# Loading the exponential's table behind the last square root of the gMLP, in a decode kernel that streams a key and value cache

## The chip, the core and the metric

The kernel runs on one core of a Trainium2 chip. The metric is the device time of one execution in microseconds (us). Before the change the median was 664.88 us of 3 runs (664.66 to 665.18).

## The reference

One layer norm, then two branches that are added to the input. Branch A is attention of one query per batch row over a cache of 4096 positions. Branch B is a small gMLP. The exponential (softmax), the GELU and the square roots (layer norms) are what the change is about.

```python
xn = _layernorm(x)                                   # a square root
q  = (xn @ wq)            # B=4, H=32, Dh=128
p  = softmax(q @ k_cache^T * Dh**-0.5)               # exponentials; k_cache 4 x 32 x 4096 x 128 bf16
A  = (p @ v_cache) @ wo
z  = gelu(xn @ w_in)                                 # GELU
z2 = _layernorm(z[..., Fh:])                         # a second square root
B  = (z[..., :Fh] * (w_sp * z2 + b_sp)) @ w_out
return x + A + B
```

The two caches are 134 MB each.

## The kernel before

The cache is cut into 16 key units and 16 value units of 8.39 MB (4 groups of 8 heads, 4 batch rows). They pass through five slots of on-chip memory, two slots to a unit, on one transfer queue: the four key units of the first group come first, then value and key units in turn. VectorE transposes a key unit in 8 steps (L361), TensorE makes the scores. After the fourth key unit of a group comes the softmax of the group, then TensorE multiplies with the value units. A new unit is issued when what lay in its slots has been used.

```python
# end of the gMLP (L316 to L332, cut)
nc.scalar.activation(out=rs[:], in_=var[:], func=ACT.Sqrt, bias=eps_t[:, 0:1], scale=1.0)   # L322
nc.vector.reciprocal(out=rs[:], in_=rs[:])                                                    # L323
# ... four more VectorE operations
etab = const.tile([P, 1], F32)
nc.scalar.activation(out=etab[:], in_=eps_t[:], func=ACT.Exp)                                 # L332

def softmax(g):
    negmax = softmax_max(g)            # row maxima: VectorE, one TensorE step, VectorE
    # ...
    for e in range(NE):                # L415
        nc.scalar.activation(out=p_bf[:, :, e, :], in_=S_ps[:, e], func=ACT.Exp, bias=negmax[:, e:e + 1], ...)
    # transpose, copies, z_fill(g, 0), z_fill(g, 1): the weights Zb of the value matmuls

def emit_V(v):                         # L444
    nc.tensor.matmul(O_ps[...], lhsT=Zb[b % 2][...], rhs=vv[...], ...)     # 64 of them
```

In the trace a table load (ACT_TABLE_LOAD) stands in front of an activation wherever the kind of function changes: square root (6.44 us), exponential (8.05), GELU (24.47), square root (26.48), exponential (122.59). None stands before the copies or before the exponentials of the later softmaxes. etab is read by nothing: it is there to have the exponential's table loaded early. The instructions are ordered by a scheduler that moves what is ready early to the front.

## Time and profile before

| | before |
|---|---|
| span of the profiled execution | 662.6 us |
| transfers | 282.25 MB, 426 GB/s over the span |
| VectorE, TensorE, ScalarE busy | 55%, 44%, 12% |
| table loads on ScalarE | 5 of 1.28 us |
| first softmax: exponential starts | 123.88 us |
| first value matmul, issue of the next value unit | 132.35, 136.00 us |

### The profile page before, as it was taken

To read this page: it belongs to the slowest core of one execution; us is meant where nothing else is said; L and a number is where in the kernel's file an instruction comes from. 1 tells how busy PE (TensorE), PEld (TensorE's weight loads), DVE (VectorE), ACT (ScalarE), POOL (GpSimd) and SP (SyncE) were. 2 spreads that over 40 slices of the span, in tenths; PEclk is the share of its full clock that TensorE was granted. 3 is DMA by queue.
4 is the path that set the end of the run, shared out by engine and by line. 5 is a ranking of instruction groups with operands and counts; after the bars stand their busy time and mean duration, and the time that the engine had idled before them with its cause. 6 is when DMAs were issued, how large, how long until landed. Compare 5 with 4: busy or idle time off the path is not lost.

```text
span 662.6 us, 5430 instructions
## 1 busy us (share of the span) xinstructions
PE 294.1 (44%) x2283; PEld 106.3 (16%) x2283; DVE 362.5 (55%) x340; ACT 79.5 (12%) x163; POOL 10.8 (2%) x35
## 2 busy tenths in 40 slices
PE   0525566266072556225446055633506254623245
PEld 0201122022021122111112022111202112211012
DVE  4338999656190849609265286745618084950002
ACT  1200000541100000530200000071110000052200
POOL 3000000000000000000000000000000000000000
PEclk9858968668577587677758596755958659667767
DMA  9999999999999999999999999999999999999996
GB/s 374 459 440 432 404 434 445 443 428 436 420 427 440 435 413 448 431 431 432 431 444 427 435 416 432 448 435 428 423 436 443 432 435 407 437 436 441 424 413 262
DMA packets 6901, 282.61 MB, mean 427 GB/s; under 512 B 808, under 2 KB 1084, under 8 KB 1500
## 3 DMA queue, kind: packets, MB, share of 16 engines
q1 hardware_dynamic: 6856, 282.25, 98.8%
q8 instruction: 18, 0.29, 0.2%
q14 instruction: 7, 0.06, 0.0%
q10 hardware_dynamic: 20, 0.01, 0.0%
HBM read 282.25 MB, written 0.01 MB: 426 GB/s over the span
## 4 chain that ended last, share of the span: by engine, by line
DMA 74%; DVE 11%; issue 11%; PE 2%; ACT 1%; SPq 0%; DVEq 0%; ACTq 0%
DMA kv<-in_A_k_cache_dram 63%; DVE kT L361 11%; DMA kv<-in_A_v_cache_dram 5%; DMA kv<-in_A_wo_dram 3%; DMA kv<-in_A_wq_dram 2%; PE O L444 2%; ACT xd L426 0%; ACT Zb L407 0%; SPq L169 0%; ACT p L415 0%; PE last_a L542 0%; DVE pT L419 0%; DVE m L379 0%; PE S L372 0%; PE misc L384 0%
## 5 line engine op out<-in xcount | busy, mean ns | idle before, releaser
L361 DVE STREAM_TRANSPOSE kT<-kv 128x2048 f32<-128x2048 f32 x128 | 282.8, 2275 | 128.5 <-DMA kv<-in_A_k_cache_dram 128.5
L372 PE MATMUL S<-kT,QZ 128*32 128x512 bf16 x1024 | 190.8, 506 | 233.3 <-DVE kT L361 233.3
L372 PEld LDWEIGHTS <-QZ 128*32 128x32 bf16 x1024 | 61.0, 111 | 357.6 <-issue 337.9
L444 PE MATMUL O<-kv,Zb 128*32 128x512 bf16 x1024 | 75.2, 458 | 58.1 <-DMA kv<-in_A_v_cache_dram 37.9
L451 DVE TENSOR_SCALAR R<-O,Mk 128x128 f32<-128x128 f32 x16 | 5.6, 351 | 122.8 <-PE O L444 122.8
L407 ACT ACTIVATE Zb<-xd,MkE 32x256 bf16<-32x256 bf16 x116 | 52.9, 498 | 108.3 <-PE O L444 106.9
L444 PEld LDWEIGHTS <-Zb 128*32 128x32 bf16 x1024 | 33.0, 113 | 99.6 <-issue 58.5
L415 ACT ACTIVATE p<-S,negmax 128x512 bf16<-128x512 f32 x8 | 5.4, 682 | 311.6 <-DVE negmax L393 311.6
L461 PE MATMUL misc<-R,SelR 128*32 128x128 f32 x32 | 6.4, 281 | 26.2 <-DVE R L453 26.2
L453 DVE SCALAR_TENSOR_TENSOR R<-O,Mk,R 128x128 f32<-128x128 f32 x48 | 16.8, 351 | 1.7
L426 DVE COPY xd<-pT 32x256 bf16<-32x256 bf16 x44 | 16.0, 364 | 0.8
L426 ACT COPY xd<-pT 32x256 bf16<-32x256 bf16 x20 | 12.2, 612 | 5.6 <-DVE pT L419 5.2
L415 ACT ACT_TABLE_LOAD x1 | 1.3, 1283 | 93.1 <-DVE negmax L393 93.1
L347 POOL COPY QZ<-qT 32x32 bf16<-32x32 bf16 x16 | 5.1, 316 | 413.4 <-PE S L372 399.8
L419 DVE STREAM_TRANSPOSE pT<-p 128x1024 bf16<-128x1024 bf16 x4 | 5.0, 1245 | 7.6 <-ACT p L415 7.6
L379 DVE TENSOR_REDUCE m<-S 128x2 f32<-128x1024 f32 x4 | 4.9, 1225 | 5.6 <-PE S L372 5.6
L461 PEld LDWEIGHTS misc<-R,SelR 128*32 128x32 f32 x32 | 2.2, 107 | 34.0 <-DVE R L453 25.3
L268 PE MATMUL q<-kv,xnT 128*32 128x512 bf16 x40 | 4.5, 631 | 5.2 <-DMA kv<-in_A_wq_dram 5.2
L384 PE MATMUL misc<-dg,ones_f 128*128 128x256 f32 x8 | 3.2, 491 | 7.5 <-DVE dg L381 7.5
L464 DVE SCALAR_TENSOR_TENSOR om<-misc,rinv,MkH 32x1024 bf16<-32x1024 f32 x4 | 5.1, 1272 | 2.0 <-PE misc L461 2.0
L430 PE MATMUL misc<-rowsum,SelP 128*32 128x2 f32 x8 | 1.1, 204 | 11.3 <-ACT p L415 11.3
L276 DVE CAST kv<-q 128x512 bf16<-128x512 f32 x1 | 0.7, 692 | 9.5 <-PE q L268 9.5
(102 smaller groups left out, 73.3 us busy)
## 6 DMA issues: line engine op xcount, KB each, us to landing
kv<-in_A_k_cache_dram SPq DMA_DIRECT2D x8, 4096.0 KB
kv<-in_A_v_cache_dram SPq DMA_DIRECT2D x1, 6144.0 KB
kv<-in_A_wq_dram SPq DMA_DIRECT2D x1, 5120.0 KB
kv<-in_A_wo_dram SPq DMA_DIRECT2D x3, 1280.0 KB
kv<-in_B_w_in_dram SPq DMA_DIRECT2D x1, 2160.0 KB, 19.9
kv<-in_A_v_cache_dram SPq DMA_DIRECT2D x1, 2048.0 KB
kv<-in_B_w_out_dram SPq DMA_DIRECT2D x1, 960.0 KB
kv<-in_A_wo_dram SPq DMA_DIRECT2D x1, 640.0 KB, 21.7
```

The source lines that it names most:

```text
L347: nc.gpsimd.tensor_copy(out=QZ[r0:r0 + 32, :, :, :, 8 + 8 * hp], in_=qT[32 * g:32 * g + 32, NE * hp:NE * hp + NE].rearrange("p e a b -> p ...
L361: nc.vector.transpose(kT[:].rearrange("p (t r) -> p t r", r=32), kw)
L372: nc.tensor.matmul(S_ps[32 * q:32 * q + 32, e], lhsT=QZ[:, b, 2 * kh + w, e, w0:w0 + 32], rhs=kb[:, i, :, e, :, w], start=(b == 0 and k < ...
L407: nc.scalar.activation(out=dst, in_=src, func=ACT.Copy, scale=mk)
L415: nc.scalar.activation(out=p_bf[:, :, e, :], in_=S_ps[:, e], func=ACT.Exp, bias=negmax[:, e:e + 1], scale=scale, accum_out=rowsum[:, e:e + 1])
L419: nc.vector.transpose(pT[:].rearrange("p t h x -> p (t h x)"), p_bf[:].rearrange("p t e m -> p (t e m)"))
L426: op(out=xd[32 * hp:32 * hp + 32, :, q, :], in_=pT[32 * q:32 * q + 32, :, hp, :].rearrange("p t x -> p x t"))
L444: nc.tensor.matmul(O_ps[32 * q:32 * q + 32, :, :], lhsT=Zb[b % 2][:, w].rearrange("p h c -> p (h c)"), rhs=vv[:, w * 4 * Dh:(w + 1) * 4 * ...
L451: nc.vector.tensor_scalar(out=R, in0=O_ps[:, 0, :], scalar1=Mk4[:, 0:1], scalar2=None, op0=ALU.mult)
L453: nc.vector.scalar_tensor_tensor(out=R, in0=O_ps[:, c, :], scalar=Mk4[:, c:c + 1], in1=R, op0=ALU.mult, op1=ALU.add)
L461: nc.tensor.matmul(oh[:], lhsT=SelR[:, b].rearrange("p h b -> p (h b)"), rhs=state["R"][:, b, :], start=(b == 0), stop=(b == B - 1))
L464: nc.vector.scalar_tensor_tensor(out=om[:], in0=oh[:, None, :].to_broadcast((G, HG, Dh)), scalar=state.pop(("rinv", g))[:, 0:1], in1=MkH[: ...
```

## The change

The intent is to have the exponential's table in place before the first softmax, where its load stood on the chain from the last scores to the first value matmul. etab reads rs, so it can't run before the second square root.

```diff
     etab = const.tile([P, 1], F32)
-    nc.scalar.activation(out=etab[:], in_=eps_t[:], func=ACT.Exp)
+    nc.scalar.activation(out=etab[:], in_=rs[:], func=ACT.Exp, scale=1e-3)
```

## The prediction

> **What bounds the kernel now.** I read the page first (busy shares and the 40 slices), then the chain that ended last, then every ScalarE instruction in order of time, and last the issue and landing times of the cache transfers around the first softmax, which is where the change acts.
>
> The page of the kernel before:
>
> ```profile
> DMA  9999999999999999999999999999999999999996
> HBM read 282.25 MB, written 0.01 MB: 426 GB/s over the span
> DMA 74%; DVE 11%; issue 11%; PE 2%; ACT 1%; SPq 0%; DVEq 0%; ACTq 0%
> ```
>
> The DMA row is at 9 in every slice but the last, so the 16 DMA engines are moving data from the first to the last slice. ScalarE is 1% of the chain. The bytes set the time: 282.25 MB at 426 GB/s are 662.6 us, the whole span. A change that moves no bytes can help only where the transfer queue runs dry, at the head, or in the tail behind the last transfers.
>
> ScalarE in order of time, kernel before (start, duration, engine, line, operation; in brackets the idle time before it and what ended it):
>
> ```profile
> 6.44 1.28 ACT L195 ACT_TABLE_LOAD   x1 [6.44 <-DVE ssq L193]
> 7.74 0.29 ACT L195 ACTIVATE rstd<-ssq,eps_t 4x1 f32<-4x1 f32 x1
> 8.05 1.28 ACT L332 ACT_TABLE_LOAD   x1
> 9.34 0.20 ACT L332 ACTIVATE etab<-eps_t 128x1 f32<-128x1 f32 x1
> 21.24 0.59 ACT L276 CAST kv<-q 128x512 bf16<-128x512 f32 x1 [11.69 <-DVE kv L276]
> 24.47 1.28 ACT L297 ACT_TABLE_LOAD   x1 [2.65 <-PE misc L291]
> ...
> 26.48 1.28 ACT L322 ACT_TABLE_LOAD   x1
> 29.21 0.29 ACT L322 ACTIVATE rs<-var,eps_t 128x1 f32<-128x1 f32 x1 [1.45 <-DVE var L319]
> 122.59 1.28 ACT L415 ACT_TABLE_LOAD   x1 [93.08 <-DVE negmax L393]
> 123.88 0.69 ACT L415 ACTIVATE p<-S,negmax 128x512 bf16<-128x512 f32 x1
> ```
>
> This shows what the author of the change saw. The preload of the exponential's table (etab, L332) stands in the source behind the gMLP, but its input eps_t is ready early, so it ran at 8.05 us, ahead of the GELU and of the second square root. Each of these loads its own table, so the exponential's is gone by 29.5 us. It is loaded again at 122.59 us, inside the first softmax, with the row maximum (negmax) done and everything waiting for the exponential. Five loads in all; no later softmax has one.
>
> **What the Trainium skill says.** "ScalarE: Activation LUTs", section "What ACT_TABLE_LOAD costs": about 1283 ns for the load and about 1380 ns for a drain, together 2.66 us for each switch of set. The trace agrees with 1283 ns (1.28 us in all five) but shows no drain beside it: negmax ends at 122.51, the load runs from 122.59 to 123.87, the exponential starts at 123.88. I use 1.28 to 1.29 us. The same page, "Table sets: the hidden batching unit", puts exp and sqrt into different sets and copies into every set. The trace agrees: the CAST at 21.24 and the copies between the later softmaxes have no load. So with etab behind the last square root nothing on ScalarE should evict the exponential's table again.
> "DMA: Bandwidth & Descriptors", section "Bandwidth", measures 425 GB/s for one large load and puts the fabric ceiling at 435 GB/s. The 426 GB/s here is at that level. (The page's 358 GB/s for HBM per core is passed here, so the measurement decides.) I therefore expect no idle bandwidth to win.
>
> **The change, part by part.**
> 1. Removed at 8.05 us: one load and one 0.20 us activation, 1.49 us of ScalarE from 8.05 to 9.54. ScalarE next has work at 21.24, which waits for VectorE. Worth 0 us.
> 2. Added behind the second square root: etab now reads rs, which the reciprocal (L323, 29.54 to 29.71) finishes. A wait on one engine did not hold back the load of L322 (it ran at 26.48, the activation waited 1.45 us more), so I expect the load at about 29.5 to 30.8 and etab of 0.20 us at about 30.8 to 31.0. ScalarE is idle from 29.5 to 122.59, and the gMLP's remaining path (L324 to L340) is VectorE and TensorE only. Nothing reads etab. Worth 0 us.
> 3. Removed at 122.59: the load in the first softmax. Four loads stay instead of five. The exponential can start at about 122.59 instead of 123.88: the softmax, the filling of Zb and the first value matmuls (132.35 us) come 1.29 us earlier. This is the only gain, and the question is whether it reaches the end.
>
> What waits for these matmuls is the issue of the next value transfer, which overwrites half of the first value unit. The trace in order of time, kernel before:
>
> ```profile
> 132.35 6.02 PE L444 MATMUL O<-kv,Zb 128*32 128x512 bf16 x64 [6.71 <-ACT Zb L407]
> ...
> 136.00 0.33 SPq L161 DMA_DIRECT2D kv<-in_A_v_cache_dram  x1
> ...
> 140.78 17.66 DVE L361 STREAM_TRANSPOSE kT<-kv 128x2048 f32<-128x2048 f32 x8 [0.84 <-DMA kv<-in_A_k_cache_dram]
> ...
> 149.70 0.33 SPq L161 DMA_DIRECT2D kv<-in_A_k_cache_dram  x1
> ...
> 160.16 3.64 PE L444 MATMUL O<-kv,Zb 128*32 128x512 bf16 x64 [0.55 <-DMA kv<-in_A_v_cache_dram]
> ...
> 179.77 17.66 DVE L361 STREAM_TRANSPOSE kT<-kv 128x2048 f32<-128x2048 f32 x8 [14.42 <-DMA kv<-in_A_k_cache_dram]
> ```
>
> The value transfer is issued at 136.00 while the key unit before it is still arriving; that lands at about 140.76. So the queue has 4.76 us of work left. The value unit lands at about 160.14, 19.4 us after the key unit; the next key unit, issued 10.4 us before its predecessor landed, lands 19.6 us after it (179.75). A unit of 8.39 MB at 427 GB/s needs 19.6 us, by calculation. The value unit lost nothing to its late issue. Issued at 134.7 it has 6.05 us of slack instead of 4.76 and lands when it did before. The sum over the three parts: 0 us.
>
> The finer windows agree: from 120 to 160 us in steps of 5 us the DMA share is 0.97 to 1.03 and the rate 410 to 446 GB/s, no dip.
>
> **The rivals.**
> a) The 1.29 us reaches the end. For it: the chain in the first softmax really is serial from the last key matmul to the first value matmul. Against it: after that the chain that ended last contains the key transfers at 108.67 to 140.76 and 149.70 to 179.75, not this softmax; and no softmax but the first had a load, so the exposed last softmax (580.6 to 593.8 us in the chain) gets nothing. Time: 664.88 - 1.29 = 663.6; with the skill's full 2.66 us it would be 662.2.
> b) The transfer issued earlier collides with the key unit in flight, which lands later, by up to the 1.29 us. For it: two transfers on the same 16 engines. Against it: the same bytes go through the same engines, and the next key issue (149.70) that hangs on that unit has 10.4 us of slack. Time: unchanged, 664.9.
> c) The new dependency makes the scheduler arrange other instructions differently, at the head above all, or puts the load in front of something that waits. For it: etab was already moved once by readiness. Against it: ScalarE has nothing else to do from 29.5 to 122.6. Where the head is touched, a loss of at most the load and etab, 1.5 us, could follow: 666.4.
> d) The load is not saved because an activation between 31 and 122 us takes another set. Nothing in the trace is there. Time: 664.9.
>
> **Range and chances.** The centre is the time before less a tenth for the small chance of (a): 664.8. The three runs before spread over 0.52 us. I allow for (a) at the low end and for another chip session and part of (c) at the high end: 663.6 to 665.9. A change of 2% would be 13.3 us, ten times the only duration that the change touches; I give 1% to each side.
>
> **What would show it right or wrong.** Right: four table loads, one of them with L332 at about 29.5 us; no load at L415; the first exponential at about 122.6; the first value matmul near 131.1; the value transfer issued near 134.7; and yet the value unit landing near 160.1 and everything after it within some tenths of where it was. Wrong at step 2: etab still early, or its load waiting on the path of L324. Wrong at step 3: the landing near 160.1 and the key landings after it (179.75, 218.46) move forward by about 1.3 us, which would mean that the queue was short of work where I read it as full.

## The result and the profile after

The changed kernel took 664.61 us (median of 6 runs, 664.48 to 664.67), the kernel before 664.85 us (6 runs, 664.40 to 665.18). The ratio is 0.9996 with a 95% interval of 0.9984 to 1.0009: the same.

The page of the changed kernel:

```profile
DMA  9999999999999999999999999999999999999996
HBM read 282.25 MB, written 0.01 MB: 426 GB/s over the span
DMA 74%; DVE 11%; issue 11%; PE 2%; ACT 1%; SPq 0%; DVEq 0%; ACTq 0%
```

The three lines are those of before to the last digit. ScalarE in order of time, changed kernel:

```profile
6.45 1.28 ACT L195 ACT_TABLE_LOAD   x1 [6.45 <-DVE ssq L193]
...
24.68 1.28 ACT L297 ACT_TABLE_LOAD   x1 [2.82 <-PE misc L291]
...
26.68 1.28 ACT L322 ACT_TABLE_LOAD   x1
29.42 0.29 ACT L322 ACTIVATE rs<-var,eps_t 128x1 f32<-128x1 f32 x1 [1.45 <-DVE var L319]
29.73 1.28 ACT L332 ACT_TABLE_LOAD   x1
31.03 0.20 ACT L332 ACTIVATE etab<-rs 128x1 f32<-128x1 f32 x1
122.93 0.69 ACT L415 ACTIVATE p<-S,negmax 128x512 bf16<-128x512 f32 x1 [91.70 <-DVE negmax L393]
```

The change did what it was meant to do. Four loads instead of five, the exponential's directly behind the square root, and none at L415. The order of the instructions on all other engines is the same in both kernels, but for a few TensorE records near 264 us that trade places.

The stretch around the first value matmul in order of time, changed kernel:

```profile
131.40 6.01 PE L444 MATMUL O<-kv,Zb 128*32 128x512 bf16 x64 [6.71 <-ACT Zb L407]
135.05 0.33 SPq L161 DMA_DIRECT2D kv<-in_A_v_cache_dram  x1
...
140.78 17.66 DVE L361 STREAM_TRANSPOSE kT<-kv 128x2048 f32<-128x2048 f32 x8 [1.79 <-DMA kv<-in_A_k_cache_dram]
...
160.15 3.64 PE L444 MATMUL O<-kv,Zb 128*32 128x512 bf16 x64 [0.54 <-DMA kv<-in_A_v_cache_dram]
```

The value matmuls start 0.95 us earlier than before (132.35) and the next value unit is issued 0.95 us earlier (136.00). But the key unit in flight is still used from 140.78 us on (it lands at 140.75) and the value unit from 160.15 on, against 160.16. VectorE's idle time before 140.78 grew from 0.84 to 1.79 us: that is where the saved time went.

The saving was 0.95 us and not 1.28 us because other things differ between two executions. The row maxima started at 119.46 us instead of 118.62 (the last score matmuls took 1.80 us instead of 1.12, with TensorE's granted clock, the share of its full speed that the chip allowed, at 0.50 instead of 1.00 from 117 to 119 us), and the small matmul among the maxima took 0.70 us instead of 1.22: 0.84 - 0.52 - 1.28 = -0.96 us.

### The profile page after: what moved, and what is told of

It is laid out like the page before. It is cut to its first block, busy times and chain, and to the rows that moved or that the text cites. A ratio compares the mean times of both kernels' runs of the same rounds, so it can differ in the third digit from the quotient of the medians.

```text
span 662.8 us, 5429 instructions
## 1 busy us (share of the span) xinstructions
PE 292.2 (44%) x2283; PEld 106.0 (16%) x2283; DVE 362.7 (55%) x340; ACT 78.2 (12%) x162; POOL 10.9 (2%) x35
## 3 DMA queue, kind: packets, MB, share of 16 engines
q1 hardware_dynamic: 6856, 282.25, 98.8%
HBM read 282.25 MB, written 0.01 MB: 426 GB/s over the span
## 4 chain that ended last, share of the span: by engine, by line
DMA 74%; DVE 11%; issue 11%; PE 2%; ACT 1%; SPq 0%; DVEq 0%; ACTq 0%
DMA kv<-in_A_k_cache_dram 63%; DVE kT L361 11%; DMA kv<-in_A_v_cache_dram 5%; DMA kv<-in_A_wo_dram 3%; DMA kv<-in_A_wq_dram 2%; PE O L444 1%; ACT xd L426 0%; ACT Zb L407 0%; ACT p L415 0%; PE last_a L542 0%; DVE pT L419 0%; DVE m L379 0%; PE misc L384 0%; PE S L372 0%; SPq L169 0%
## 5 line engine op out<-in xcount | busy, mean ns | idle before, releaser
L415 ACT ACTIVATE p<-S,negmax 128x512 bf16<-128x512 f32 x8 | 5.4, 683 | 403.3 <-DVE negmax L393 403.3
```

## The experiments

Theory: the queue of transfers has work left when the value unit is issued, so the issue can move by some slack without any effect. Rivals: (1) the gain is real but is eaten by the new load at the head; (2) the softmax isn't tied to the end at all, or a load is hidden whatever stands around it; (3) each us in the softmax counts. Against one comparison alone all of these can be made to fit "same". Times of before: 664.59 us (9 runs) for e1 to e4, 664.61 (9) for e5 to e8, 664.57 (9) for e9 and e10. Each experiment has 5 runs (e1, e5, e7, e10) or 4 (the others). All results were correct.

| run | what | time us (lowest to highest) | ratio to before, 95% | value issue us |
|---|---|---|---|---|
| e1 | no etab | 664.74 (664.54 to 665.18) | 1.0001 (0.9988 to 1.0013) | |
| e5 | first softmax, 1 activation | 664.98 (664.61 to 665.22) | 1.0003 (0.9991 to 1.0016) | 135.84 |
| e2 | first softmax, 3 | 666.06 (665.38 to 666.55) | 1.0018 (1.0003 to 1.0033) | 139.60 |
| e3 | first softmax, 5 | 669.39 (668.88 to 669.93) | 1.0070 (1.0056 to 1.0083) | 142.28 |
| e6 | first softmax, 9 | 675.47 (675.08 to 675.93) | 1.0162 (1.0147 to 1.0178) | 148.79 |
| e7 | last softmax, 3 | 664.55 (664.51 to 664.58) | 0.9998 (0.9985 to 1.0010) | 603.63 |
| e4 | last softmax, 5 | 665.72 (665.58 to 666.24) | 1.0016 (1.0002 to 1.0029) | 607.75 |
| e8 | last softmax, 13 | 678.03 (677.73 to 678.44) | 1.0201 (1.0187 to 1.0215) | 621.03 |
| e9 | before, with 36 copies | 670.39 (669.51 to 671.56) | 1.0091 (1.0076 to 1.0107) | 142.80 |
| e10 | after, with 36 copies | 668.57 (668.30 to 669.78) | 1.0061 (1.0048 to 1.0073) | 141.82 |

"Value issue" is the issue behind the first value matmuls (after: 135.05) or, for e4, e7 and e8, behind those of the last group (after: 599.24).

### e1: without etab

```diff
-    etab = const.tile([P, 1], F32)
-    nc.scalar.activation(out=etab[:], in_=eps_t[:], func=ACT.Exp)
```

> The kernel before without etab at all: part 1 of the change alone. The load stays in the first softmax (four loads, the last at L415 near 122.6 us). Slack theory (the value transfer's issue has 4 to 6 us to spare, so nothing in the first softmax counts): same as both kernels, 664.4 to 665.2 us. Rival 'the gain is real and is eaten by the new load at the head': here the head has one load less than after and the softmax one more, so it would be 1.3 us slower than after, 665.9, if the softmax load counted, or 1.3 us faster than after, 663.3, if the head load counted.

The load in the softmax is still there, e1 in order of time:

```profile
122.72 1.28 ACT L415 ACT_TABLE_LOAD   x1 [92.97 <-DVE negmax L393]
```

664.74 us: neither 665.9 nor 663.3. Rival (1) falls: there are not two effects of 1.3 us that cancel. The early load of the kernel before was worth nothing that shows, within 0.9 us.

### e2, e3, e5, e6: more loads in the first softmax

The same edit with n = 3, 5, 1 and 9, on the changed kernel:

```diff
+    def switches(m, g):
+        for i in range(n if g == 0 else 0):
+            nc.scalar.activation(out=sw[:, i:i + 1], in_=m[:, 0:1], func=ACT.Exp if i % 2 else ACT.Sqrt, bias=eps_t[:, 0:1], scale=0.0)
+        return m
-        negmax = softmax_max(g)
+        negmax = switches(softmax_max(g), g)
```

Square root and exponential in turn force a load for each. The expectations of e2 and e3, which ran first:

> The changed kernel with three tiny activations (Sqrt, Exp, Sqrt, scale 0) between the row maximum and the exponential of the first softmax: four table loads there, the first of them perhaps ahead of the wait, so a delay of 4.7 us (3 loads of 1.28 and 3 activations of 0.29) to 6.0 us on that softmax. Slack theory: the issue moves from 135.05 to 139.8 to 141, about when the key unit in flight lands (140.75); time plus 0 to 2 us. Rival 'the softmax is not tied to the end': 0. Rival 'every us in it counts': plus 4.7 to 6.0.

> The same with five tiny activations: delay 7.9 to 9.2 us. Slack theory: issue near 143 to 144, queue empty from 140.75, time plus 2.2 to 5.5 us, and the value unit lands that much later than 160.1. Rival 'not tied': 0. Rival 'every us counts': plus 7.9 to 9.2.

e2 came out 1.47 us and e3 4.80 us above before: both inside what the slack theory expected, both outside of rivals (2) and (3). Luck has a part in these hits: the delays came out shorter than expected (issues at 139.60 and 142.28 us instead of 139.8 to 141 and 143 to 144), and the slack did too. With a queue that is empty from 140.75 us, these issues should have cost nothing and 1.5 us. Windows of 1 us show where the transfers stop. Busy time of each engine, then TensorE's clock, DMA share and GB/s; changed kernel first, then e3:

```profile
138.00:139.00 1.00, 0.00 (x0) 0.00 (x0) 0.91 (x3) 0.97 (x3) 0.00 (x0) 1.00 1.67 721
139.00:140.00 1.00, 0.38 (x2) 0.23 (x3) 0.00 (x0) 0.98 (x3) 0.00 (x0) 0.83 0.61 262
140.00:141.00 1.00, 0.00 (x0) 0.00 (x0) 0.23 (x1) 0.97 (x3) 0.00 (x0) 0.50 1.06 459
```

```profile
137.00:138.00 1.00, 0.00 (x0) 0.00 (x0) 0.90 (x4) 0.95 (x3) 0.00 (x0) 0.50 0.60 262
138.00:139.00 1.00, 0.37 (x4) 0.14 (x8) 0.32 (x3) 0.97 (x3) 0.00 (x0) 0.50 0.01 0
...
142.00:143.00 1.00, 1.00 (x16) 0.43 (x12) 0.00 (x0) 0.29 (x1) 0.00 (x0) 0.59 0.00 0
143.00:144.00 1.00, 1.00 (x28) 0.41 (x16) 0.00 (x0) 0.00 (x0) 0.00 (x0) 1.00 3.14 1049
```

(A window counts a packet, whole, where it starts. A packet of the caches is 64 KB, and it takes 2.4 us: 0.60 of 16 engines and 262 GB/s in 1 us are four of them. So single rates above the mean mean little, and a zero says that no packet starts, not that none moves.) In e3 no packet of the caches starts from 138 to 143 us. In the changed kernel there is no such stretch. When I set up the next runs I read this as "nothing moves from 138.0 us on, and the first packet of the value unit comes 0.7 us after its issue", which put the last safe issue at about 137.3 us, and the expectations of the next two runs say so.

The packet records in the traces, which the views don't print, correct this reading. Each of the 16 DMA engines works through its own packets, and they finish the key unit one after another:

| run | issue | first engine without a packet | last packet of the key unit ends | first packet of the value unit | idle time, mean of 16 engines | span above 662.8 us |
|---|---|---|---|---|---|---|
| e2 | 139.60 | 138.1 | 139.9 | 140.56 | 2.1 | 1.6 |
| e3 | 142.28 | 138.3 | 140.1 | 143.24 | 4.5 | 4.6 |
| e6 | 148.79 | 138.0 | 140.0 | 149.75 | 11.1 | 10.9 |
| e9 | 142.80 | 138.1 | 139.8 | 143.76 | 5.1 | 4.9 |
| e10 | 141.82 | 138.0 | 139.8 | 142.78 | 4.1 | 3.9 |

(The idle time is summed over the stretch around the issue, from the engines' packets of the cache transfers' queue. 662.8 us is the span of the changed kernel; e9 and e10 are told below.) In the changed kernel and in the one before, the same count gives 0.0 us. In all five runs of the table the first value packet starts 0.96 us after the issue. So the last issue that leaves no engine without a packet is at 138.0 to 138.3 less 0.96, or 137.0 to 137.3 us: nearly the first figure, for another reason. A later issue costs at first only what a part of the engines lose, and the time is longer by about the engines' mean idle time.

> One tiny Sqrt in the first softmax: one load exposed there, as in the kernel before, plus 0.29 us, so a delay of 1.6 us against the changed kernel. The runs so far put the last issue time that leaves no hole in the transfers at about 137.2 us (in e2 and e3 no packet moves from 138.0 until about 0.7 us after the issue). Slack theory with this smaller slack: issue at 136.0 to 136.7, so 0 to 0.3 us: 664.5 to 665.1. Every us counts: plus 1.6, 666.2.

> Nine tiny activations in the first softmax: delay 14.2 us. Slack theory: the issue moves from 135.05 to about 149, 12 us behind the last safe time; less what the end gave back in e2 and e3 (up to 1 us): plus 11 to 12.3, 675.6 to 676.9. Against e3 (four loads and four activations fewer, 6.3 us) plus 6.3 us, that is one to one. Not tied: 664.6. Recovery later (the rest of the kernel catches up): well under plus 10.

e5, with an issue at 135.84 as in the kernel before (136.00), is the same as before. e6 is 10.86 us above before, a little under what was expected (675.47 us, the range began at 675.6), and 6.08 us above e3 for four more loads and activations (6.3 us by their durations). Issue time less extra time gives the issue from which the loss counts: e2 139.60 - 1.47 = 138.1, e3 137.5, e6 137.9. Well beyond that, each us costs about one.

The loads themselves, e5 in order of time on ScalarE:

```profile
31.15 1.28 ACT L333 ACT_TABLE_LOAD   x1
122.12 0.29 ACT L333 ACTIVATE sw<-negmax,eps_t 128x1 f32<-128x1 f32 x1 [89.69 <-DVE negmax L393]
122.42 1.28 ACT L415 ACT_TABLE_LOAD   x1
123.72 0.69 ACT L415 ACTIVATE p<-S,negmax 128x512 bf16<-128x512 f32 x1
```

The load for the square root ran at 31.15 us, ahead of its activation's wait by 91 us. So of n + 1 loads only n delay the softmax. In the kernel before, the load at L415 did wait for negmax: there a separate wait instruction of L415 stands before the load (one at 122.5 us in the records of that line). The loads of L195 and L297, which waited too, also have one; that of L322, which ran ahead, has none.

### e4, e7, e8: the same in the last softmax

The edit with `g == 3` and n = 5, 3 and 13. The chain that ended last contains this softmax, so reading it literally makes each us count.

> The same five activations in the last softmax instead of the first: delay 7.9 to 9.2 us in a stretch that the chain that ended last does contain. Slack theory: the value issue behind it (599.24) has 11.7 us until the transfer in flight lands (610.96), so 0, within 0.5 us. Reading the chain literally: plus 7.9 to 9.2 us.

> Three tiny activations in the last softmax: delay 4.7 us, issue of the value transfer near 604, 3.4 us ahead of the last safe time there (610.96 less 3.5 = 607.4). Slack theory: 0 to 0.3 us. Reading the chain that ended last literally: plus 4.7. If the 1.1 us of e4 came from something that scales with any delay in the last softmax, plus 0.6.

> Thirteen tiny activations in the last softmax: delay 20.4 us, issue near 620, 12.5 us behind the last safe time. Slack theory: plus 12 to 13.5 us, 676.6 to 678.1. Reading the chain literally: plus 20.4.

The issue of a value unit and the matmuls that use that unit, for e7, e4 and e8 in order of time:

```profile
603.63 14.01 SPq L161 DMA_DIRECT2D kv<-in_A_v_cache_dram  x3
630.45 6.27 PE L444 MATMUL O<-kv,Zb 128*32 128x512 bf16 x64 [11.66 <-DMA kv<-in_A_v_cache_dram]
```

```profile
607.75 10.66 SPq L161 DMA_DIRECT2D kv<-in_A_v_cache_dram  x3
630.70 5.23 PE L444 MATMUL O<-kv,Zb 128*32 128x512 bf16 x64 [11.14 <-DMA kv<-in_A_v_cache_dram]
```

```profile
621.03 6.38 SPq L161 DMA_DIRECT2D kv<-in_A_v_cache_dram  x3
642.86 5.64 PE L444 MATMUL O<-kv,Zb 128*32 128x512 bf16 x64 [14.30 <-DMA kv<-in_A_v_cache_dram]
```

In the changed kernel these are 599.24 and 630.40. In e7 the issue is 4.4 us later and the use is not: the time is that of before. The literal reading of the chain (plus 4.7) falls. e8 is 13.4 us above before, as expected.

e4 is a miss of the first expectation: 0 within 0.5 us was expected, 1.13 us came. Its issue moved by 8.5 us, to 607.75. By the packet records the first value packet then starts at 608.72, while the first DMA engines had run out from about 606.1 to 606.4 us on (e4 and e8). So there was no moment without any packet, but the engines' mean idle time from 606 to 610 us was about 1.2 us, the size of the loss. The last safe issue here was therefore near 605.2 us, not 607.4. The value unit is used only 0.3 us later; the rest shows further on, where the first part of the last value unit is used at 646.29 us instead of 645.18. In e8 the value unit is 12.5 us late and the part after it 13.7 (658.91); its engines' mean idle time is 14.0 us. e7, whose issue left no engine idle, has neither. How the loss passes from one unit to the next was not followed.

### e9, e10: the change itself where nothing is to spare

Both kernels got 36 small copies between the row maximum and the exponential of the first softmax. No table load stands before the copies in either trace, so the only difference between e9 and e10 is the diff of this study.

```diff
+        for i in range(36 if g == 0 else 0):
+            nc.scalar.activation(out=sw[:, i], in_=ident_f[:, 0:32], func=ACT.Copy, scale=m[:, 0:1])
```

> The kernel before with 36 small copies (128x32, no table of their own, estimated 0.22 to 0.30 us each from the other ScalarE rows, so 8 to 11 us) between the row maximum and the exponential of the first softmax: a queue that runs dry there in any case. The load of the exponential's table still stands behind the copies. Slack theory: time plus 7 to 10 us, and 1.0 to 1.6 us more than e10. If the load is hidden whatever stands around it: equal to e10.

> The changed kernel with the same 36 copies: the change itself on a ground without slack. Slack theory: time plus 5.5 to 9 us, 1.28 us (1.0 to 1.6) less than e9, so the change is worth its full load here. If the load is hidden whatever stands around it: equal to e9.

ScalarE in order of time, e9 and then e10:

```profile
122.07 7.73 ACT L333 ACTIVATE sw<-ident_f,negmax 128x32 bf16<-128x32 f32 x36 [92.43 <-DVE negmax L393]
129.81 1.28 ACT L415 ACT_TABLE_LOAD   x1
131.10 0.69 ACT L415 ACTIVATE p<-S,negmax 128x512 bf16<-128x512 f32 x1
```

```profile
122.08 7.73 ACT L333 ACTIVATE sw<-ident_f,negmax 128x32 bf16<-128x32 f32 x36 [90.97 <-DVE negmax L393]
129.72 0.67 ACT L415 ACTIVATE p<-S,negmax 128x512 bf16<-128x512 f32 x1
```

The exponential starts 1.38 us earlier in e10 (129.72 against 131.10), and here the time follows: 668.57 us against 670.39, 1.8 us by the medians and 1.7 us by the means, with intervals that don't touch (1.0048 to 1.0073 and 1.0076 to 1.0107), though one run of e10 (669.78) lies above one of e9 (669.51). The two profiled executions differ by 1.0 us (spans 666.7 and 667.7), as does the idle time of their DMA engines (4.1 and 5.1 us): of the 1.38 us 0.98 reach the issue, since TensorE took 3.65 us from the first value matmul to the issue in e10 and 3.22 in e9. So the runs of these two kernels scatter by as much as the effect's excess over 1.3 us; I don't read anything into that excess. Issue time less extra time, as above, is 137.0 us for e9 and 137.8 us for e10. Rival (2), a load that is hidden whatever stands around it, falls. Both totals stayed below what I expected (4.0 and 5.8 us instead of 5.5 to 9 and 7 to 10). The copies took 7.73 us together and not 8 to 11, and in e10 they began at 122.08 us, 0.85 us before the exponential of the changed kernel (122.93), so the issue came only 6.8 us later than without them.

No experiment points to a version that beats both kernels: neither has a hole in its transfers at this place, so there is nothing to close.

## Why the prediction was right

Predicted were 664.8 us, from 663.6 to 665.9; measured were 664.61.

- **The bound.** Right. 282.25 MB at 426 GB/s stayed the time, and the three page lines are unchanged.
- **Parts 1 and 2, the removed early load and the new one.** Right: load at 29.73 (29.5 predicted), ahead of etab's wait, nothing on the path of L324 moved by it. e1 shows no effect of either, within 0.9 us.
- **Part 3, the load taken out of the softmax.** Right in its mechanism, and 0 was right as its worth: the value unit's use moved from 160.16 to 160.15. The next two key landings came 0.24 and 0.25 us earlier (179.51 and 218.21), far from the 1.3 us that would have meant a queue short of work; by 257.33 us (257.34 before) nothing of it is left. e9 and e10 show that the load counts, with 1.0 to 1.8 us, once the slack is gone.
- **The slack was mis-sized.** This is the term that was off. I put it at 4.76 us, from the issue (136.00) to the landing of the key unit (140.76). The experiments and their packet records put the last harmless issue at 137.0 to 137.3 us, so the kernel before had 1.0 to 1.3 us and the changed one has 2.0 to 2.3. The step that failed is "so the queue has 4.76 us of work left". It counts to the landing, which is the last of 16 reports, one from each DMA engine: in e3 these come from 138.56 to 140.64 us, 0.3 to 0.5 us behind the end of an engine's last packet. The engines run out from 138.0 to 138.3 us on, some 2.6 us before the landing, and the first packet starts 0.96 us after the issue; take both from 4.76 and about 1.2 are left. The error did no harm here, since any slack above zero makes the saving worthless, and in that the prediction had some luck: a quarter of the slack that I counted was there. In a kernel whose softmax were 3 us longer the queue would have run dry, and my figure would have said that it didn't.
- **Rival (a), the last softmax "exposed".** I called it exposed because the chain contains it. e7 shows that 4.4 us more there cost nothing; it has some 6 us of slack (599.24 to about 605.2). A transfer in that chain runs from issue to landing: 29.8 us for a key unit whose bytes need 19.6. Most of the other 10 us is waiting behind the unit before it, and the chain doesn't mark that.
- **Rival (b), a collision.** Not seen: the key unit landed at 140.75 us as before (140.76).
- **Rival (c), another order.** Not seen at the head: only ScalarE's order changed, and the few TensorE records near 264 us.
- **Rival (d), another load.** Not seen: four loads.

## What to carry to other kernels

A wait taken off an engine's chain is worth something only if a transfer, or whatever sets the end, starts later because of it: find the issue that hangs on the chain and see whether the packets ahead of it run out before the new ones begin. Measure that slack from the first packet of the new transfer, not from its issue, to the moment at which the first DMA engine runs out of packets, not to the landing. Know how a view books a packet before you read a zero as standstill. Don't take each step of the chain that ended last for exposed. If a result is "same", delay the same place on purpose by two or three sizes: a flat part and then a slope of one tells slack from a place that doesn't matter.

## What the Trainium skill lacked or had wrong

- "ScalarE: Activation LUTs", "What ACT_TABLE_LOAD costs": 1283 ns for a load is what the loads here took, but the drain of about 1380 ns beside it didn't show. In e3, five activations with loads between them follow each other every 1.60 us (122.18, 123.78, 125.37 us), which is 1.28 for the load, 0.29 for the activation and 0.03 between, not 2.66 us for a switch.
- No page that I read says that a load can run far ahead of its activation's wait (31.15 against 122.12 us in e5) or is held back when a separate wait instruction precedes it (122.59 us in the kernel before). It decides whether a switch of tables costs anything.
- "DMA: Bandwidth & Descriptors", "Where 436 GB/s comes from": it says that for loads from HBM the side of the HBM binds, at about 358 GB/s. This kernel's one core passes that with 426 GB/s over the whole span. The sentence lacks the condition that the same page gives in "Measured", that both cores of a pair are loading.
